# Seven block products instead of eight for chunks 12 to 15 as well, with the weight mixes made by copying and accumulating DMAs

## The chip, the cores and the metric

The kernel runs on one core of one Trainium2 chip. The metric is the device time of one execution in microseconds, lower is better. Several executions are taken and their median is given; one more is profiled.

## What is computed

The reference is a linear attention with decaying state (4 sequences, 8 heads, 768 steps, head size 48), followed by a mixture of four experts, each a two-layer network, over all 3072 rows:

```python
for t in range(S):                       # r, k, v: [4, 8, 768, 48]
    cur = einsum('bhd,bhe->bhde', u * kt, vt)
    y[:, :, t] = einsum('bhd,bhde->bhe', rt, state + cur)
    state = w * state + einsum('bhd,bhe->bhde', kt, vt)

p = domain_probs / (domain_probs.sum(-1, keepdims=True) + 1e-09)
for e in range(4):                       # x: y as [3072, 384]
    h = maximum(x @ w1[e], 0)            # [3072, 1024]
    out += p[:, e:e+1] * (h @ w2[e])     # [3072, 384]
```

## The kernel before

**Chunks and groups.** The 768 steps of each of the 4 sequences are cut into 6 chunks of 128 rows, so there are 24 chunks; chunk `ci` is step block `ci // 4` of sequence `ci % 4`. Attention runs chunk by chunk: K and R are scaled by powers of the decay (`scale`, VectorE), transposed (by a DMA transpose from chunk 8 on), multiplied into scores (`At`, TensorE), masked (`mask`, VectorE), multiplied with V (`Y`, TensorE) and completed with a diagonal term (`ruk`, `dv`, GpSimd; `Yout`, VectorE). A state update (`Sm` on TensorE, `Sv` on VectorE, `S` on GpSimd) feeds the chunk four places later. The experts work on groups of four chunks, `sc` = 0 to 5.

**The standard expert.** For groups 0 to 3 (`FIRST = 4`), layer one (`hT_ps`, lines 640 and 646) makes the hidden rows transposed, ScalarE applies ReLU (line 657), layer two (`out_ps`, line 678) takes 8 matmuls of 384 columns for each chunk and expert, and ScalarE (first expert) or VectorE (line 689, the other three) weighs the result by `p` and adds it into the output tile `oacc`.

**The seven-product form.** For groups 4 and 5 the weight `p` is multiplied into the attention row instead (`Xs`, lines 533 and 535, four scaled copies of a chunk; since `p` is not negative, ReLU lets it through). Then layer two is one product with the four experts joined in the contraction, and `products` (called for each pair of chunks, `q` = 0 or 1) makes it by a scheme of the Strassen kind: two chunks times two column halves of 192, with the contraction split in even and odd blocks. Seven products replace eight; each is 16 matmuls of 192 columns (`M_ps`, line 807), in two halves `hf` of two experts. Five of the seven need a sum or difference of hidden blocks (`sum`, line 790, 10 for each pair, VectorE), which is held in one of eight buffers S0 to S7 (four lie in the former staging area, four in the `RK` tiles of attention). Five need a mixed weight (`mix`, line 741, VectorE, one for each of 4 experts): mixes 6, 7 and 1 go into free input tiles, mixes 3 and 4 overwrite a quarter of `w2_sb`. The results are added into `oacc` on VectorE (lines 822 and 834) and copied there on ScalarE (line 828). All seven products of a group wait until layer one of the whole group is done, since the hidden rows of all four experts are needed; they then fill the whole tile `hAll`.

**The order of work.** Every piece is a job with a name, the engines that may do it with a booked time, what it needs, a rank (lower goes first) and slots that it takes or drops. A simulation in the kernel's Python code plays all jobs at the booked times and so gives the order in which each engine's instructions are issued; on the chip each engine runs its own list in order and waits on semaphores. `GATES` names for each pair of chunks from 8 on the layer-one job before which its attention may not begin. Loads are issued from SP in a fixed order, and stores, transposes and the other DMAs are on SP's queue too.

```python
job(("mix", e, what), {"V": 0.62}, run, needs, TOTC + 0.1 * e, (("inp", TOTC + e),) if tag else ())
```

Here `{"V": 0.62}` is the engine and the booked time. `("inp", ...)` is a slot of the input tiles.

Of the kernel before, what the change touches and what calls it, by code (L numbers as in the profile page):

```python
# [14 lines left out]
ALU = mybir.AluOpType  # L15
# [4 lines left out]
def kernel(  # L20
# [65 lines left out]
    spin_in = consts.tile([128, 128], BF16)  # L86
# [35 lines left out]
    for b in range(B):  # L122
        for i in range(2):
# [3 lines left out]
    wC = consts.tile([128, NP], F32)  # L127
    p_nat = consts.tile([128, E, TOTC], F32)
# [8 lines left out]
    GATES = (3, 5, 6, 7, 9, 10, 11, 12)  # L137
# [9 lines left out]
    FIRST = 4  # L147
# [4 lines left out]
                 mm=4, xTe=3, hTs=3, oacc=6, Yse=1)  # L152
    slots.update({f"{n}{i}": 1 for n, m in (("xTs", 2), ("h", 4), ("S", 8)) for i in range(m)})
# [178 lines left out]
    def attention(ci):  # L332
# [55 lines left out]
        job(("Vb", ci), {"A": 0.42} if ci < SUB else {"P": 0.5}, vb, [("Vt", ci)],  # L388
# [121 lines left out]
        def yout():  # L510
            if plain:
                tl["Ysb", ci] = work.tile([128, HD], BF16, tag="Ysb", bufs=3, name="Ysb")
# [9 lines left out]
        if dmat and plain:  # L522
            job(("Xout", ci), {"S": 1.2}, lambda: nc.sync.dma_start_transpose(
                get_xTe(sc)[:, :, ci % B, :], tl["Ysb", ci]), [("Yout", ci)], -5.0,
                (("xTe", sc),), (("Ysb", ci),), (0.45, 24))
        elif dmat:
            n_p = b * NCH + c

            def xs(e):
                def run(eng):  # L530
                    o = y_e[:, e * HD:(e + 1) * HD]
                    if eng == "A":
                        nc.scalar.mul(o, tl["Ysb", ci], p_nat[:, e, n_p:n_p + 1])
                    else:
                        nc.vector.tensor_scalar(o, tl["Ysb", ci], scalar1=p_nat[:, e, n_p:n_p + 1],  # L535
                                                scalar2=None, op0=ALU.mult)
                return run
            for e in range(E):
                job(("Xs", ci, e), {"A": 0.61, "V": 0.51}, xs(e), [("Yout", ci)] + all_cast, rk - 0.7,
                    (("Yse", ci),) if e == 0 else (), (("dv", ci),), behind=(("Xs", ci, 0),) if e else ())  # L540
            job(("Xout", ci), {"S": 1.3}, lambda: nc.sync.dma_start_transpose(
                get_xTe(sc)[:, :, ci % B, :], y_e),
                [("Xs", ci, e) for e in range(E)] + all_cast, -5.0,
                ((f"xTs{sc % 2}", sc),), (("Yse", ci),), (1.8, 96))
        else:
            tag = "mm" if ci < SUB else "tr"

            def x():
                ps = tl["X", ci] = psum.tile([128, NDB, 128], BF16, tag=tag,
                                             bufs=4 if tag == "mm" else 1, name="xT_ps")  # L550
                for db in range(NDB):
                    nc.tensor.transpose(ps[:, db, :], tl["Ysb", ci][:, db * 128:(db + 1) * 128], ident)  # L552
            job(("X", ci), {"T": 0.17}, x, [("Yout", ci)], on_pe - 1, ((tag, "X", ci),), (("Ysb", ci),))
# [18 lines left out]
        def sv():  # L572
            ps = tl["Sp", ci]
            if c:
                a = 1664 + ci % 2 * NP * D
                tl["Tn", ci] = early[:, a:a + NP * D].rearrange("p (q d) -> p q d", d=D)
# [15 lines left out]
        if c == 0:  # L592
            job(("S", ci), {"V": 0.56}, sv, [("Sm", ci), ("Yout", SUB - 1)], rk + 2, (), (("ys", "S", ci),))
        else:
            job(("Sv", ci), {"V": 0.56}, sv, [("Sm", ci)], rk - 0.1, (), (("ys", "S", ci),))
            job(("S", ci), {"P": 1.1}, sp, [("Sv", ci)], rk - 0.5)

    y_e = stg_b[:, 16384:16384 + E * HD]
# [27 lines left out]
    def moe(k, e, sc, single):  # L626
# [4 lines left out]
        for g, (fb, s0, n) in enumerate(groups):  # L631
# [19 lines left out]
            def relu(fb=fb, s0=s0, n=n):  # L651
# [10 lines left out]
                [("S", ci) for ci in range(TOTC - 2 * SUB, TOTC - SUB) if sc == FIRST and not e] +  # L662
# [48 lines left out]

    def oacc(ci):
        if ("oacc", ci // 2) not in tl:
            tl["oacc", ci // 2] = big.tile([128, 2, Dm], F32, tag="oacc", bufs=6, name="oacc")
        return tl["oacc", ci // 2][:, ci % 2, :]

    def store(ci, needs, a=0, bb=Dm):
        job(("st", ci, a), {"S": 0.5}, lambda: nc.sync.dma_start(
            out[row0(ci):row0(ci) + C, a:bb], oacc(ci)[:, a:bb]), needs, -6.0, (),
# [7 lines left out]
    def mix(e, what):  # L727
        v = b_of(e)
        B11, B12, B21, B22 = (v[:, :, j, h * DH:(h + 1) * DH] for j in range(2) for h in range(2))
        x, y, op = {1: (B11, B22, ALU.add), 6: (B11, B12, ALU.add), 7: (B21, B22, ALU.add),  # L730
                    3: (B12, B22, ALU.subtract), 4: (B21, B11, ALU.subtract)}[what]
        tag = {6: "Rt", 7: "Kt", 1: "Vt"}.get(what)

        def run(eng):
            if tag:
                o = work.tile([128, H, D], F32, tag=tag, bufs=NIN, name=tag)
                o = tl["mix", e, what] = o.rearrange("p h d -> p (h d)").bitcast(BF16).rearrange(
                    "p (i d) -> p i d", d=DH)
            else:
                o = x  # L740
            (nc.vector if eng == "V" else nc.gpsimd).tensor_tensor(o, x, y, op=op)
        needs = [("cast", 2, e, i) for i in range(NPC)]
        if what in (3, 4):
            needs += [("mix", e, 9 - what if what == 3 else 7)]
            needs += [("l2", e, ci) for ci in range(FIRST * SUB)]
        else:
            needs += [("Vt", TOTC - 1), ("Xout", TOTC - 1)]
        job(("mix", e, what), {"V": 0.62}, run, needs, TOTC + 0.1 * e, (("inp", TOTC + e),) if tag else ())

    for e in range(E):  # L750
        for what in (6, 7, 1, 3, 4):
            mix(e, what)
# [7 lines left out]
    s_no, s_tok = [0], {}  # L760
    s_free = [("T", ci, 1) for ci in range(TOTC - NRK, TOTC)]

    def products(sc, q, at0):
# [3 lines left out]
        def a_of(j, s, hf):  # L767
            return hAll[:, (1 - hf) * 2 * NFB + j:(2 - hf) * 2 * NFB:2, s, :]

        SUMS = {1: ((0, s1), (1, s2), ALU.add), 2: ((0, s2), (1, s2), ALU.add),  # L770
                5: ((0, s1), (1, s1), ALU.add), 6: ((0, s2), (0, s1), ALU.subtract),
                7: ((1, s1), (1, s2), ALU.subtract)}
# [3 lines left out]
        for n, m in enumerate(ORDER_P):  # L776
            at = at0 + 2.0 * n / 7
            for hf in range(2):
                needs = list(relus[hf])
                if m in SUMS:  # L780
                    x, y, op = SUMS[m]
                    no = s_no[0] % 8
                    s_no[0] += 1
                    if no < 4:
                        S = stg_b[:, 12288 + no * 1024:12288 + (no + 1) * 1024]
                    else:
                        S = RKB[no - 4].rearrange("p i h d -> p (i h d)")
                    S = tl["S", sc, q, m, hf] = S.rearrange("p (i c) -> p i c", c=128)
                    job(("sum", sc, q, m, hf), {"V": 0.74},
                        lambda S=S, x=x, y=y, op=op, hf=hf: nc.vector.tensor_tensor(  # L790
                            S, a_of(*x, hf), a_of(*y, hf), op=op),
                        relus[hf] + all_cast + s_free, at - 60, ((f"S{no}", sc, q, m, hf),), hts[hf])
                    s_tok[sc, q, m, hf] = (f"S{no}", sc, q, m, hf)
                    needs = [("sum", sc, q, m, hf)]
                w_ready = [("mix", e, m) for e in (2 * hf, 2 * hf + 1)] if m not in (2, 5) else []

                def mm(m=m, hf=hf):
# [14 lines left out]
                    behind=(("P", sc, q, m, 0),) if hf else ())  # L812
# [30 lines left out]
            elif m == 5:  # L843
                job(("C", sc, q, 5, 0), {"V": 0.33}, add(0, 0, ALU.subtract), ready + [("C", sc, q, 1, 0)], r, (), drop)
                job(("C", sc, q, 5, 1), {"V": 0.33}, add(0, 1, ALU.add), ready + [("C", sc, q, 3, 0)], r, (), drop)
# [217 lines left out]
```

## Time and profile before

| | us |
|---|---|
| median of 3 runs | 292.45 (291.52 to 294.41) |
| profiled execution, own time | 291.22 |
| its span, first to last instruction | 289.4 |
| TensorE busy | 282.9 (98%) |
| VectorE busy | 196.2 (68%) |
| ScalarE busy | 155.8 (54%) |
| GpSimd busy | 106.0 (37%) |

The span leaves out 1.8 us of the profiled execution's own time. A busy figure adds the durations of the engine's instructions. Matmuls overlap in TensorE's pipeline, so a group's mean duration (326 ns for a matmul of 384 columns) is longer than the distance from one start to the next; for a sum of work, the distance (the pitch) is the figure to use. In the lines, L with a number is a line of the kernel before; PE is TensorE, PEld its weight load, DVE is VectorE, ACT is ScalarE, POOL is GpSimd, SP is SyncE.

### The profile page before, as it was taken

The numbers are of one execution on the slowest core, as the hardware profiler recorded it, in microseconds if no ns is written. First come the engines' busy times: TensorE is split into PE (matmuls) and PEld (weight loads), VectorE is DVE, ScalarE is ACT, GpSimd is POOL, SyncE is SP. The second block draws the span as 40 slices with busy tenths as digits, with TensorE's granted clock in tenths as the row PEclk, the third lists the DMA queues.
The fourth block names the chain that finished last, engine by engine and source line by source line (L and its number), as shares of the span: only waits on it lengthen the run. The fifth ranks groups of instructions, "written<-read, shape, count | busy, mean of one in ns | idle before, by whom it ended". The sixth has DMA issues, their size and how long they took to land.

```text
span 289.4 us, 6324 instructions
## 1 busy us (share of the span) xinstructions
PE 282.9 (98%) x2482; PEld 181.0 (63%) x2482; DVE 196.2 (68%) x382; ACT 155.8 (54%) x262; POOL 106.0 (37%) x138
## 2 busy tenths in 40 slices
PE   7989999999999999999999999999999999999995
PEld 3777556865955554555555655555544699544995
DVE  5977976797569969674989875554793387120883
ACT  4673968647845243455455466554469701689210
POOL 2875244564979695667567132000000000000000
PEclk9999999999999999999999999999999999999999
DMA  7999999999995898979399556223110001100011
GB/s 152 248 283 271 320 305 269 187 316 202 239 184 112 158 223 191 209 159 179 79 187 194 121 127 111 57 51 60 54 57 0 0 29 40 45 1 2 0 57 54
DMA packets 120418, 40.05 MB, mean 138 GB/s; under 512 B 108458, under 2 KB 120364, under 8 KB 120388
## 3 DMA queue, kind: packets, MB, share of 16 engines
q1 hardware_dynamic: 120372, 39.64, 59.1%
q8 instruction: 19, 0.31, 0.4%
q14 instruction: 11, 0.09, 0.1%
q10 hardware_dynamic: 16, 0.00, 0.0%
HBM read 26.79 MB, written 4.72 MB: 109 GB/s over the span
## 4 chain that ended last, share of the span: by engine, by line
PE 91%; SPq 4%; DMA 3%; issue 0%; DVE 0%; ACT 0%
PE hT_ps L646 38%; PE out_ps L678 28%; PE M_ps L807 13%; PE hT_ps L640 5%; SPq L201 3%; DMA Vt<-in_v_dram 3%; PE At_ps L463 2%; PE Y_ps L501 2%; PE Y_ps L494 1%; PE St_ps L567 1%; SPq L214 1%; DMA xTe<-Ysb 1%; PE RKT_ps L421 1%; PE xT_ps L552 0%; PE p_ps L309 0%
## 5 line engine op out<-in xcount | busy, mean ns | idle before, releaser
L657 ACT ACTIVATE hAll<-hT_ps 128x512 bf16<-128x512 f32 x168 | 99.6, 597 | 73.2 <-PE hT_ps L646 67.7
L678 PE MATMUL out_ps<-w_sb,hAll 128*128 128x384 bf16 x512 | 92.9, 326 | 0.0
L646 PEld LDWEIGHTS <-w_sb 128*128 128x128 bf16 x504 | 46.9, 98 | 49.9 <-DMA xTe<-Ysb 0.8
L646 PE MATMUL hT_ps<-xTe,w_sb 128*128 128x512 bf16 x312 | 77.0, 379 | 0.3 <-DMA xTe<-Ysb 0.3
L678 PEld LDWEIGHTS <-hAll 128*128 128x128 bf16 x512 | 48.6, 98 | 34.0
L689 DVE SCALAR_TENSOR_TENSOR oacc<-out_ps,p_nat,oacc 128x384 f32<-128x384 f32 x48 | 29.4, 616 | 26.2 <-PE out_ps L678 25.6
L646 PE MATMUL hT_ps<-stg,w_sb 128*128 128x512 bf16 x192 | 42.4, 379 | 0.0
L372 POOL TENSOR_TENSOR ruk<-Rt,Kt 128x384 f32<-128x384 f32 x24 | 25.1, 1048 | 30.8 <-DMA Rt<-in_r_dram 17.8
L472 DVE TENSOR_TENSOR AtM<-At_ps,mask 128x512 bf16<-128x512 f32 x48 | 30.7, 681 | 1.4 <-PE At_ps L463 1.3
L398 POOL TENSOR_TENSOR dv<-Vt,dcoef 128x384 f32<-128x384 f32 x24 | 21.3, 889 | 15.3 <-DVE stg L535 7.4
L790 DVE TENSOR_TENSOR RK<-hAll 128x1024 bf16<-128x1024 bf16 x20 | 13.1, 686 | 18.7 <-ACT hAll L657 18.6
L380 POOL TENSOR_TENSOR ruk<-ruk,U_sd 128x384 f32<-128x384 f32 x23 | 25.2, 1097 | 0.8
L588 POOL TENSOR_TENSOR S<-hAll,wC 64x192 bf16<-64x192 f32 x32 | 17.4, 545 | 9.7 <-DVE hAll L583 8.5
L790 DVE TENSOR_TENSOR stg<-hAll 128x1024 bf16<-128x1024 bf16 x20 | 13.1, 686 | 9.7 <-ACT hAll L657 9.5
L640 PE MATMUL hT_ps<-xTe,w_sb 128*128 128x128 bf16 x288 | 18.0, 219 | 0.4 <-ACT w_sb L78 0.2
L640 PEld LDWEIGHTS <-w_sb 128*128 128x128 bf16 x288 | 16.6, 98 | 1.0 <-ACT w_sb L78 0.4
L82 POOL CAST Vb<-Vt 128x384 bf16<-128x384 f32 x20 | 11.6, 581 | 13.6 <-DMA Vt<-in_v_dram 5.3
L359 DVE TENSOR_TENSOR RK<-Kt,W_sd 128x384 bf16<-128x384 f32 x20 | 16.5, 830 | 0.0
L655 ACT ACTIVATE hAll<-hT_ps 128x512 bf16<-128x512 f32 x24 | 14.1, 596 | 4.2 <-PE hT_ps L640 3.3
L687 ACT ACTIVATE oacc<-out_ps,p_nat 128x384 f32<-128x384 f32 x16 | 9.2, 579 | 12.5 <-PE out_ps L678 8.8
L393 DVE TENSOR_REDUCE dcoef<-ruk 128x8 f32<-128x384 f32 x24 | 13.1, 545 | 3.4 <-POOL ruk L380 3.0
L828 ACT COPY oacc<-M_ps 128x384 f32<-128x384 f32 x8 | 3.8, 479 | 19.6 <-PE M_ps L807 19.6
(89 smaller groups left out, 298.4 us busy)
## 6 DMA issues: line engine op xcount, KB each, us to landing
stg<-in_moe_w_dram SPq DMA_DIRECT2D x16, 576.0 KB, 6.6
Kt<-in_k_dram SPq DMA_DIRECT2D x24, 192.0 KB, 3.8
Vt<-in_v_dram SPq DMA_DIRECT2D x24, 192.0 KB, 3.9
Rt<-in_r_dram SPq DMA_DIRECT2D x24, 192.0 KB, 4.3
out_dram<-oacc SPq DMA_DIRECT2D x23, 192.0 KB, 1.9
stg<-in_moe_w_dram SPq DMA_DIRECT2D x8, 384.0 KB, 6.6
RKT<-RK SPq DMA_TRANSPOSE x16, 3.3
out_dram<-oacc SPq DMA_DIRECT2D x2, 96.0 KB, 1.6
```

The source lines that it names most:

```text
L372: nc.gpsimd.tensor_mul(tl["ruk", ci], tl["Rt", ci], tl["Kt", ci])
L380: nc.gpsimd.tensor_mul(tl["ruk", ci], tl["ruk", ci], U_sd)
L398: nc.gpsimd.tensor_mul(tl["dv", ci], tl["Vt", ci], tl["dcoef", ci].to_broadcast((128, H, D)))
L472: nc.vector.tensor_mul(tl["AtM", ci][:, j], tl["At", ci, j], mask[:, None, :].to_broadcast((128, NP, C)))
L588: nc.gpsimd.tensor_mul(S_new[pr, :, cl], tl["Tn", ci][pr], wC[pr, :, None].to_broadcast((P2, NP, D)))
L640: nc.tensor.matmul(ps[:, i, :], w1_sb[:, e, db, (fb + i) * 128:(fb + i + 1) * 128], xTe[:, db, s0, :], start=(i == 0 and db == 0), stop=(i ...
L646: nc.tensor.matmul(ps[:, 0:n, :].rearrange("p a b -> p (a b)"), w1_sb[:, e, db, fb * 128:(fb + 1) * 128], xTe[:, x0 + db, s0:s0 + n, :].re ...
L657: nc.scalar.activation(hTs[:, fb, s0:s0 + n, :], ps[:, 0:n, :], AF.Relu)
L678: nc.tensor.matmul(ps, relu_tile(e, sc)[:, fb, s, :], w2_sb[:, e, fb, :], start=(fb == 0), stop=(fb == NFB - 1))
L689: nc.vector.scalar_tensor_tensor(oacc(ci), in0=tl["o", e, ci], scalar=pe, in1=oacc(ci), op0=ALU.mult, op1=ALU.add)
L790: lambda S=S, x=x, y=y, op=op, hf=hf: nc.vector.tensor_tensor(S, a_of(*x, hf), a_of(*y, hf), op=op),
L807: nc.tensor.matmul(tl["P", sc, q, m], st, moving(m, e, i), start=(hf == 0 and n == 0), stop=(hf == 1 and n == 7))
```

## The change

Group 3 (chunks 12 to 15) goes over to the seven-product form: `FIRST` becomes 3. The signs of the scheme are turned: all sums of hidden blocks become differences, and four of the five weight mixes become sums, which a DMA can make by adding into its destination. A mix is now made for two experts at once. Mix 1 stays on VectorE as a difference. Mixes 7 and 6 are made by a copying DMA from SP and an accumulating DMA from GpSimd, both within SBUF, into output tiles and layer-one input tiles that are free by then. Mixes 4 and 3 are accumulated in place in `w2_sb` by one DMA from GpSimd each, once the standard layer two of groups 0 to 2 is done with the experts concerned.

Around it: in the new group the sums have six buffers, four in the staging area, one in the `Ysb` tiles and one in an output tile (the `RK` tiles are still in use by attention then); the sums for the first pair are ordered with four of them ahead. All sums are chained in a fixed order, and so are all products. The state's temporary `Tn` gets its own tile, the gates of five pairs of chunks move, V copies from chunk 8 on may be made on ScalarE too, and the scaled copies `Xs` rank later.

```diff
-    GATES = (3, 5, 6, 7, 9, 10, 11, 12)
+    GATES = (3, 6, 6, 3, 9, 11, 13, 15)
-    FIRST = 4
+    FIRST = 3
+    MIX_RANK = 13.0
+    XS_ON = {"A": 0.61, "V": 0.51}
+    MIX_ON = {"V": 1.5}
+    VB_ON = {'A': 0.42, 'P': 0.5}
+    XS_RANK = 1.0
+    SUM_RANK = -60
...
-        job(("Vb", ci), {"A": 0.42} if ci < SUB else {"P": 0.5}, vb, [("Vt", ci)],
+        job(("Vb", ci), {"A": 0.42} if ci < SUB else {"P": 0.5} if ci < 8 else VB_ON, vb, [("Vt", ci)],
...
-                [("S", ci) for ci in range(TOTC - 2 * SUB, TOTC - SUB) if sc == FIRST and not e] +
...
+    o_sb = weights.tile([128, 6, 2, Dm], F32)
+    o_free, o_at, o_left = list(range(6)), {}, {}
...
+    def mix_by_dma(what, hf):
+        home = ({1: 0, 7: 1, 6: 2}.get(what), hf)
+        where = None if what in (3, 4) else "oacc" if home in ((0, 0), (0, 1), (1, 0)) else "xTe"
+        j1, h1, j2, h2 = quarters(what)
+        both = w2_sb[:, 2 * hf:2 * hf + 2].rearrange("p e (i j) d -> p (e i) j d", j=2)
+        x, y = (both[:, :, j, h * DH:(h + 1) * DH] for j, h in ((j1, h1), (j2, h2)))
...
+        cast = [("cast", 2, e, i) for e in (2 * hf, 2 * hf + 1) for i in range(NPC)]
+        if where == "oacc":
+            needs = cast + [("ev", E - 1, ci) for ci in range(2 * SUB)]
         else:
+            needs = cast + [("l1", E - 1, FIRST - 1 if home == (2, 1) else 1, NFB - 1, 0)]
+        if what == 1:
+            job(("mix", 1, hf), MIX_ON, lambda eng: (nc.vector if eng == "V" else nc.gpsimd).tensor_tensor(
+                out_of(), x, y, op=ALU.subtract), needs, MIX_RANK, ((where, "mix", home),))
+            return
+        if where:
+            job(("mixc", what, hf), {"S": 0.5}, lambda: nc.sync.dma_start(out_of(), x), needs, 900.0,
+                ((where, "mix", home),), (), (2.6, 64))
+            needs = [("mixc", what, hf)]
+        else:
+            needs = [("mix", 6 if what == 3 else 7, hf)]
+            needs += [("l2", e, ci) for ci in range(FIRST * SUB) for e in (2 * hf, 2 * hf + 1)]
+        job(("mix", what, hf), {"P": 1.2}, lambda eng: nc.gpsimd.dma_start(
+            out_of() if where else x, y, accum_op=ALU.add), needs, MIX_RANK)
+
+    for what in (1, 7, 6, 4, 3):
+        for hf in range(2):
+            mix_by_dma(what, hf)
...
+        homes = (0, 1, 2, 3, 8, 9) if sc == FIRST else (0, 1, 2, 3, 4, 5, 6, 7)
+        ahead = 0 if q else len(homes) - 2
+        seq_s = [(m, 0) for m in with_sum[:ahead]]
+        for n, m in enumerate(with_sum):
+            seq_s += [(m, 1)] if ahead else [(m, 0), (m, 1)]
+            if ahead and n + ahead < len(with_sum):
+                seq_s.append((with_sum[n + ahead], 0))
...
+                lambda S=S, x=x, y=y, key=(sc, q, m, hf): nc.vector.tensor_tensor(
+                    s_of(S, key), a_of(*x, key[3]), a_of(*y, key[3]), op=ALU.subtract),
...
-                w_ready = [("mix", e, m) for e in (2 * hf, 2 * hf + 1)] if m not in (2, 5) else []
+                w_ready = [("mix", m, hf)] if m not in (2, 5) else []
```

More of the change, by code (lines that the diff above doesn't have):

```diff
@@ L85 @@
     nc.scalar.preload_act_table_set("natural_log_exp_and_others")
-    spin_in = consts.tile([128, 128], BF16)
+    spin_in = early[:, 1664:1728].bitcast(BF16)
     nc.vector.memset(spin_in, 1.0)
@@ L127 @@
     wC = consts.tile([128, NP], F32)
+    Tn = consts.tile([128, NP, D], F32)
     p_nat = consts.tile([128, E, TOTC], F32)
@@ L151 @@
     slots = dict(inp=NIN, wst=NST, RKT=4, AtM=2, Ysb=3, ruk=3, dv=3, Vb=4, At=2, tr=1, ys=1,
-                 mm=4, xTe=3, hTs=3, oacc=6, Yse=1)
-    slots.update({f"{n}{i}": 1 for n, m in (("xTs", 2), ("h", 4), ("S", 8)) for i in range(m)})
+                 mm=4, xTe=3, hTs=3, oacc=6, Yse=1, Tn=1)
+    slots.update({f"{n}{i}": 1 for n, m in (("xTs", 2), ("h", 4), ("S", 10)) for i in range(m)})
     jobs = {}
@@ L511, in yout @@
             if plain:
-                tl["Ysb", ci] = work.tile([128, HD], BF16, tag="Ysb", bufs=3, name="Ysb")
+                y_at[ci] = y_free.pop(0)
+                tl["Ysb", ci] = y_sb[:, y_at[ci] * HD:(y_at[ci] + 1) * HD]
             else:
@@ L522, in attention, with x_dma @@
         if dmat and plain:
-            job(("Xout", ci), {"S": 1.2}, lambda: nc.sync.dma_start_transpose(
-                get_xTe(sc)[:, :, ci % B, :], tl["Ysb", ci]), [("Yout", ci)], -5.0,
+            def x_dma():
+                nc.sync.dma_start_transpose(get_xTe(sc)[:, :, ci % B, :], tl["Ysb", ci])
+                y_free.append(y_at[ci])
+            job(("Xout", ci), {"S": 1.2}, x_dma, [("Yout", ci)], -5.0,
                 (("xTe", sc),), (("Ysb", ci),), (0.45, 24))
@@ L538, in attention @@
             for e in range(E):
-                job(("Xs", ci, e), {"A": 0.61, "V": 0.51}, xs(e), [("Yout", ci)] + all_cast, rk - 0.7,
+                job(("Xs", ci, e), XS_ON, xs(e), [("Yout", ci)] + all_cast, rk + XS_RANK,
                     (("Yse", ci),) if e == 0 else (), (("dv", ci),), behind=(("Xs", ci, 0),) if e else ())
@@ L552, in x @@
                     nc.tensor.transpose(ps[:, db, :], tl["Ysb", ci][:, db * 128:(db + 1) * 128], ident)
+                y_free.append(y_at[ci])
             job(("X", ci), {"T": 0.17}, x, [("Yout", ci)], on_pe - 1, ((tag, "X", ci),), (("Ysb", ci),))
@@ L574, in sv @@
             if c:
-                a = 1664 + ci % 2 * NP * D
-                tl["Tn", ci] = early[:, a:a + NP * D].rearrange("p (q d) -> p q d", d=D)
+                tl["Tn", ci] = Tn
             for j in range(2):
@@ L594, in attention @@
         else:
-            job(("Sv", ci), {"V": 0.56}, sv, [("Sm", ci)], rk - 0.1, (), (("ys", "S", ci),))
-            job(("S", ci), {"P": 1.1}, sp, [("Sv", ci)], rk - 0.5)
+            job(("Sv", ci), {"V": 0.56}, sv, [("Sm", ci)], rk - 0.1, (("Tn", ci),), (("ys", "S", ci),))
+            job(("S", ci), {"P": 1.1}, sp, [("Sv", ci)], rk - 0.5, (), (("Tn", ci),))
+    y_sb = weights.tile([128, 3 * HD], BF16)
+    y_free, y_at = [0, 1, 2], {}
     y_e = stg_b[:, 16384:16384 + E * HD]
@@ L710, in moe, with run @@
                 store(ci, [("ev", e, ci)])
+    o_sb = weights.tile([128, 6, 2, Dm], F32)
+    o_free, o_at, o_left = list(range(6)), {}, {}
     def oacc(ci):
         if ("oacc", ci // 2) not in tl:
-            tl["oacc", ci // 2] = big.tile([128, 2, Dm], F32, tag="oacc", bufs=6, name="oacc")
+            o_at[ci // 2] = o_free.pop(0)
+            tl["oacc", ci // 2] = o_sb[:, o_at[ci // 2]]
         return tl["oacc", ci // 2][:, ci % 2, :]
     def store(ci, needs, a=0, bb=Dm):
-        job(("st", ci, a), {"S": 0.5}, lambda: nc.sync.dma_start(
-            out[row0(ci):row0(ci) + C, a:bb], oacc(ci)[:, a:bb]), needs, -6.0, (),
+        o_left[ci // 2] = o_left.get(ci // 2, 0) + 1
+        def run():
+            nc.sync.dma_start(out[row0(ci):row0(ci) + C, a:bb], oacc(ci)[:, a:bb])
+            o_left[ci // 2] -= 1
+            if not o_left[ci // 2]:
+                o_free.append(o_at[ci // 2])
+        job(("st", ci, a), {"S": 0.5}, run, needs, -6.0, (),
             (("oacc", ci // 2),), (0.5 if bb - a == Dm else 0.3, 8))
@@ L725, in b_of @@
         return w2_sb[:, e].rearrange("p (i j) d -> p i j d", j=2)
[L727 to L745, printed above, removed]
-        else:
-            needs += [("Vt", TOTC - 1), ("Xout", TOTC - 1)]
-        job(("mix", e, what), {"V": 0.62}, run, needs, TOTC + 0.1 * e, (("inp", TOTC + e),) if tag else ())
@@ L750, with quarters, out_of @@
-    for e in range(E):
-        for what in (6, 7, 1, 3, 4):
-            mix(e, what)
+    def quarters(what):
+        return {1: (0, 0, 1, 1), 6: (0, 0, 0, 1), 7: (1, 0, 1, 1), 3: (0, 1, 1, 1), 4: (1, 0, 0, 0)}[what]
+    def mix_by_dma(what, hf):
[4 more added lines that the diff above has]
+        x, y = (both[:, :, j, h * DH:(h + 1) * DH] for j, h in ((j1, h1), (j2, h2)))
+        def out_of():
+            if ("mixed", home) not in tl:
+                if where == "oacc":
+                    u = o_sb[:, o_free.pop(0)].rearrange("p s d -> p (s d)").bitcast(BF16)
+                else:
+                    u = big.tile([128, NDB, SUB, 128], BF16, tag="xTe", bufs=3, name="w_mix")
+                    u = u.rearrange("p a s c -> p (a s c)")
+                tl["mixed", home] = u.rearrange("p (i d) -> p i d", d=DH)
+                for i in range(2):
+                    tl["mix", 2 * hf + i, what] = tl["mixed", home][:, 4 * i:4 * i + 4, :]
+            return tl["mixed", home]
+        cast = [("cast", 2, e, i) for e in (2 * hf, 2 * hf + 1) for i in range(NPC)]
+        if where == "oacc":
+            needs = cast + [("ev", E - 1, ci) for ci in range(2 * SUB)]
+        else:
+            needs = cast + [("l1", E - 1, FIRST - 1 if home == (2, 1) else 1, NFB - 1, 0)]
[7 more added lines that the diff above has]
+            needs = [("mixc", what, hf)]
+        else:
+            needs = [("mix", 6 if what == 3 else 7, hf)]
+            needs += [("l2", e, ci) for ci in range(FIRST * SUB) for e in (2 * hf, 2 * hf + 1)]
+        job(("mix", what, hf), {"P": 1.2}, lambda eng: nc.gpsimd.dma_start(
+            out_of() if where else x, y, accum_op=ALU.add), needs, MIX_RANK)
@@ L758, in moving @@
         return {2: v[:, i, 0, 0:DH], 3: v[:, i, 0, DH:Dm], 4: v[:, i, 1, 0:DH], 5: v[:, i, 1, DH:Dm]}[m]
-    s_no, s_tok = [0], {}
+    s_no, s_tok, s_last, p_last = [0] * NSC, {}, [None], [None]
+    y_over = [("Xout", ci) for ci in range(FIRST * SUB)]
     s_free = [("T", ci, 1) for ci in range(TOTC - NRK, TOTC)]
@@ L768, in a_of @@
             return hAll[:, (1 - hf) * 2 * NFB + j:(2 - hf) * 2 * NFB:2, s, :]
-        SUMS = {1: ((0, s1), (1, s2), ALU.add), 2: ((0, s2), (1, s2), ALU.add),
-                5: ((0, s1), (1, s1), ALU.add), 6: ((0, s2), (0, s1), ALU.subtract),
-                7: ((1, s1), (1, s2), ALU.subtract)}
+        SUMS = {1: ((0, s1), (1, s2)), 2: ((0, s2), (1, s2)), 5: ((0, s1), (1, s1)),
+                6: ((0, s2), (0, s1)), 7: ((1, s1), (1, s2))}
         relus = [[("relu", e, sc, fb, 0) for e in (2 * hf, 2 * hf + 1) for fb in range(NFB)]
@@ L775, in products @@
         hts = [tuple((h_tag(e, sc), e, sc) for e in (2 * hf, 2 * hf + 1)) for hf in range(2)]
-        for n, m in enumerate(ORDER_P):
-            at = at0 + 2.0 * n / 7
-            for hf in range(2):
[L779 to L794, printed above, removed]
-                w_ready = [("mix", e, m) for e in (2 * hf, 2 * hf + 1)] if m not in (2, 5) else []
@@ new lines, in products @@
+        homes = (0, 1, 2, 3, 8, 9) if sc == FIRST else (0, 1, 2, 3, 4, 5, 6, 7)
+        at_of = {m: at0 + 2.0 * n / 7 for n, m in enumerate(ORDER_P)}
+        with_sum = [m for m in ORDER_P if m in SUMS]
+        ahead = 0 if q else len(homes) - 2
[4 more added lines that the diff above has]
+                seq_s.append((with_sum[n + ahead], 0))
@@ new lines, in s_of @@
+        def s_of(S, key):
+            if S is None:
+                if "s_pair" not in tl:
+                    tl["s_pair"] = o_sb[:, o_free.pop(0)].rearrange("p s d -> p (s d)").bitcast(BF16)[:, 0:1024]
+                S = tl["S", *key] = tl["s_pair"].rearrange("p (i c) -> p i c", c=128)
+            return S
+        for m, hf in seq_s:
+            x, y = SUMS[m]
+            no = homes[s_no[sc] % len(homes)]
+            s_no[sc] += 1
+            if no < 4:
+                S = stg_b[:, 12288 + no * 1024:12288 + (no + 1) * 1024]
+            elif no < 8:
+                S = RKB[no - 4].rearrange("p i h d -> p (i h d)")
+            else:
+                S = y_sb[:, 0:1024] if no == 8 else None
+            if S is not None:
+                S = tl["S", sc, q, m, hf] = S.rearrange("p (i c) -> p i c", c=128)
+            job(("sum", sc, q, m, hf), {"V": 0.74},
+                lambda S=S, x=x, y=y, key=(sc, q, m, hf): nc.vector.tensor_tensor(
+                    s_of(S, key), a_of(*x, key[3]), a_of(*y, key[3]), op=ALU.subtract),
+                relus[hf] + all_cast + (s_free if 4 <= no < 8 else y_over if no == 8 else []),
+                at_of[m] + SUM_RANK, ((f"S{no}", sc, q, m, hf),) + ((("oacc", "S"),) if no == 9 else ()), hts[hf],
+                behind=(s_last[0],) if s_last[0] else ())
+            s_last[0] = ("sum", sc, q, m, hf)
+            s_tok[sc, q, m, hf] = (f"S{no}", sc, q, m, hf)
@@ L797, in mm @@
+        for m in ORDER_P:
+            at = at_of[m]
+            for hf in range(2):
+                needs = [("sum", sc, q, m, hf)] if m in SUMS else list(relus[hf])
+                w_ready = [("mix", m, hf)] if m not in (2, 5) else []
                 def mm(m=m, hf=hf):
@@ L811, in products @@
                     hts[hf] + ((s_tok[sc, q, m, hf],) if m in SUMS else ()),
-                    behind=(("P", sc, q, m, 0),) if hf else ())
+                    behind=(p_last[0],) if p_last[0] else ())
+                p_last[0] = ("P", sc, q, m, hf)
             def o_of(m=m):
@@ L843, in products @@
             elif m == 5:
-                job(("C", sc, q, 5, 0), {"V": 0.33}, add(0, 0, ALU.subtract), ready + [("C", sc, q, 1, 0)], r, (), drop)
-                job(("C", sc, q, 5, 1), {"V": 0.33}, add(0, 1, ALU.add), ready + [("C", sc, q, 3, 0)], r, (), drop)
+                job(("C", sc, q, 5, 0), {"V": 0.33}, add(0, 0, ALU.add), ready + [("C", sc, q, 1, 0)], r, (), drop)
+                job(("C", sc, q, 5, 1), {"V": 0.33}, add(0, 1, ALU.subtract), ready + [("C", sc, q, 3, 0)], r, (), drop)
             elif m == 7:
```

## The prediction

> **What bounds the kernel now.** I read the page from the top: busy shares, the rows of 40 slices, the chain that ended last; then the chain in order of time for the last third, the stretches cut at its borders, and the groups of the lines that the diff touches.
>
> ```profile
> PE 282.9 (98%) x2482; PEld 181.0 (63%) x2482; DVE 196.2 (68%) x382; ACT 155.8 (54%) x262; POOL 106.0 (37%) x138
> ...
> PE   7989999999999999999999999999999999999995
> ...
> PE 91%; SPq 4%; DMA 3%; issue 0%; DVE 0%; ACT 0%
> ```
>
> A busy TensorE alone proves little, so the chain is read next: 91% of it is TensorE, and from 109 us on there is nothing else until the last addition.
>
> ```profile
> 211.20 1.30 PE out_ps L678 x8
> 212.50 16.19 PE hT_ps L646 x75
> 228.68 18.48 PE M_ps L807 x224
> 247.16 20.72 PE hT_ps L646 x96
> 267.88 18.50 PE M_ps L807 x224
> 286.38 0.02 issue
> 286.40 0.35 DVE oacc L822
> ```
>
> Columns: start, length, what, how many. Each block's length over its count is the pitch: 20.72 / 96 = 215.8 ns (512 columns), 18.48 / 224 = 82.5 ns (192 columns), 1.30 / 8 = 162.5 ns (384 columns). Both seven-product blocks have the same pitch throughout, so TensorE never waits for a sum or a mixed weight there. The waits of TensorE agree: none over 1.1 us, and that one is at the start. So the end moves by the matmul time taken out, less any new TensorE stall.
>
> The other engines, cut at the same borders (PE, PEld, DVE, ACT, POOL busy, clock, DMA share, GB/s):
>
> ```profile
> 130.00:170.00 40.00, 40.00 (x338) 22.71 (x335) 32.46 (x62) 20.90 (x37) 21.45 (x30) 1.00 0.72 144
> 170.00:212.50 42.50, 42.50 (x277) 23.09 (x276) 24.43 (x47) 23.45 (x41) 3.46 (x5) 1.00 0.38 78
> 212.50:228.68 16.18, 16.18 (x77) 7.39 (x76) 7.33 (x14) 14.32 (x24) 0.00 (x0) 1.00 0.04 13
> 228.68:247.16 18.48, 18.48 (x226) 18.42 (x224) 14.46 (x29) 2.51 (x5) 0.00 (x0) 1.00 0.09 34
> ```
>
> VectorE is the second busiest: 81% while attention and standard layers run, 78% in a seven-product block. Today those two never meet: GpSimd has done with attention at 178 us, the first such block starts at 228.68. After the change they do meet.
>
> **What the Trainium skill says.** (1) "TensorE: Matmul & The Clock Gate", Back-to-back issue gap, gives N / 2.4 + 2.5 ns for warm matmuls in isolation and warns that weight loads can make it longer at small N; the trace has 82.5 and 162.5 ns, the formula's 82.5 and 162.5, with no such penalty. (2) "DMA: Bandwidth & Descriptors", SWDGE vs HWDGE vs iDMA: an accumulating transfer can only be issued from GpSimd, whose cores write the descriptors; the section Anatomy of one DMA fits about 2.0 us + bytes / 436 kB per us. No transfer of the kernel before is of this kind, so nothing here confirms it. (3) "SBUF — State Buffer", Who interferes with whom: a VectorE instruction with two SBUF inputs shuts out GpSimd reads. The trace agrees in kind: the GpSimd product L380 runs from 992 to 1512 ns. (4) The DMA page's rules for kernel authors: another access to the bytes of an accumulate must wait for its semaphore. So products 3 and 4 cannot start before their in-place transfers land.
>
> **The change part by part.**
>
> *TensorE.* Chunks 12 to 15 lose the standard second layer, 4 chunks x 4 experts x 8 = 128 matmuls at 162.5 ns = 20.80 us, and gain 2 pairs x 7 products x 16 = 224 at 82.5 ns = 18.48 us. Saved: 2.32 us. Layer one and attention keep their counts. No stall of size is left to recover after the start (the trace shows one of 0.4 us near 109 us), so 2.3 us is close to the most that the change can give.
>
> *ScalarE.* Out: 4 first evictions at 579 ns (L687), 2.3 us. In: 4 copies at 479 ns and its share of 16 scalings at 606 ns (L533). In the pure layer-one stretch it has 14.32 of 16.18 us busy, nearly all ReLU (24 at 597 ns); work put there would delay TensorE through the four PSUM buffers. The scalings of chunks 12 to 15 come earlier, where ScalarE is half idle (20.90 of 40): I cost them at nothing. Without that cover each would be 0.6 us.
>
> *VectorE.* Out: 12 additions at 616 ns = 7.4 us, and 20 mixes at 551 ns = 11.0 us. In: 20 sums at 686 ns = 13.7 us; result additions 12 x 352 + 2 x 554 ns = 5.3 us; two mixes of doubled size, estimated from the 551 ns row at 1.0 us each; up to 16 scalings at 412 ns = 6.6 us, less ScalarE's share. Sum about +5 us of 196: harmless as a total. The place matters. When the last chunk of 8 to 11 has left the second layer, TensorE has three experts of layer one left, 24 x 648 ns = 15.5 us, then the 18.5 us block. In the 15.5 us VectorE has four advance sums (2.7), attention of chunks 20 and 21 and their scalings. One chunk there costs 0.83 + 0.72 (scale) + 2 x 0.68 (mask) + 0.55 + 0.55 = 4.0 us, its scalings 1.6 if all here: 14.0 of 15.5. In the block: the 14.5 us of today's block, of 18.5. Chunks 22 and 23 want another 11.3 us. Over both stretches 39.8 us of work stands against 34.0, and 5.8 must slide into the following layer-one stretch, where today's twin of it has only 2.85 us of VectorE work in 20.7. It may slide: these chunks are not read until layer one of chunks 20 to 23, some 40 us later, and sums outrank attention (SUM_RANK -60). Only six sum buffers instead of eight stand in this block; walking the order, a sum needs the buffer of a product two ahead, and each arrives 0.3 us or more before use. I take 1 us of stalls for the block, bounds 0 and 4.
>
> *Weight mixes.* Ten jobs for two experts each: two on VectorE, four copies from SP, eight accumulations from GpSimd (for 7, 6, 4 and 3). Each transfer has 128 x 8 runs of 384 bytes, 1024 packets, as many as an input load (192 kB in 192-byte runs).
>
> ```profile
> q1 hardware_dynamic: 120372, 39.64, 59.1%
> ...
> Kt<-in_k_dram SPq DMA_DIRECT2D x24, 192.0 KB, 3.8
> ```
>
> 0.591 x 16 x 289.4 us / 120372 = 22.7 ns a packet; 64 packets an engine = 1.5 us, landing at 3.8. An accumulation reads two and writes one: low bound like a plain load, 3.8 us; high bound twice the packet time and GpSimd held throughout, 1.5 + 3.8 = 5.3 us each with the next one behind it. The skill's fit gives 2.0 + 393 / 436 = 2.9 us. I take 4.5 us to landing and about 1.2 us on GpSimd (the figure that the diff's plan books; bounds 1.0 and 5.3). For mixes 7 and 6 this is hidden: used 15 us or more later. Mixes 4 and 3 for experts 2 and 3 may start only after that last second-layer matmul, so 15.5 us before use; two in a row take under 10. On GpSimd, 4 x 1.2 = 4.8 us join 21.45 of 40; ahead of a dv or S there, an issue delays Y, but the wait has room. The copies stand last in SP's order, behind loads and transposes. SP also carries four transposes of four times the size for chunks 12 to 15; a DMA share of 0.72 leaves room.
>
> *The rest.* The gates let chunks 20 to 23 begin only with layer one of chunks 12 to 15 (experts 1 and 3), near 170 and 180 us; today their score matmuls run at 163 and 186 us. Their rows are wanted at about 245, so the delay costs nothing unless it crowds the block (C). V copies of chunks 8 to 23 (0.5 us) may go to ScalarE; it has room there. Removing the 24-fold wait on old S jobs, the fixed Tn tile, the hand-kept y_sb and o_sb: bookkeeping. Four of six output slots go to mixes and sums; two pairs then share two slots 20 us apart, and a store takes 1.9 us.
>
> Sum: 291.22 - 2.3 + 1.0 = 289.9 for the profiled execution; the median of the runs shown lies 1.23 above it: 291.2 us.
>
> **Rivals.**
> *VectorE full (C).* If attention of chunks 22 and 23 lands inside the block instead of sliding, 14.5 + 8.0 = 22.5 us stand against 18.5: 4 us of stall at worst, about 3 with part of it elsewhere. For it: 78% today without any attention. Against: the ranks. 292.45 - 2.3 + 3 = 293.1.
> *Accumulations late (B), the slower side.* Place: between the last second-layer matmul of chunks 8 to 11 and product 3. If the four in-place accumulations run one behind the other on GpSimd, the point of decision is 15.5 / 4 = 3.9 us each. At the 5.3 bound the last lands 21.2 us after, 5.7 late; with smaller stalls through GpSimd before, 6.5: 292.45 - 2.3 + 6.5 = 296.7. For it: the plan counts the mixed weight as there 0.17 us after the issue, which no transfer of the page does. Against: experts 0 and 1 are free earlier, so only two need stand in line.
>
> **How the numbers follow.** Forecast 0.48, C 0.24, B 0.28. A measurement of this kernel tells about 1%, 2.9 us, from no change. The forecast lies within it, apart from 0.04 beyond on the fast side, since 2.3 saved can hardly be 2.9. C is within for 0.16 and slower for 0.08. B is slower. Faster 0.04, same 0.60, slower 0.36. Range: from 289.6, full saving and a little more, to 298.5, B with some GpSimd delay on top. The forecast's own range is 289.8 to 292.6.
>
> **What would show it.** 672 matmuls at L807's successor with 82.5 ns pitch, 384 at L678's; a block of 224 near 187 to 206 us lasting 18.5 us plus its stalls. Waits of TensorE on VectorE sums in this block speak for C; waits on an accumulating DMA before the first product for B; GpSimd instructions over 1.2 us at the DMA issues would break my price. Stalls of TensorE before 165 us would mean that the new order of attention costs what I took as free, and that the forecast is wrong.

## The result, and the profile after

The changed kernel takes 312.38 us (median of 4 runs, 310.87 to 313.06), the kernel before 292.43 us beside it: ratio 1.0665, interval 1.0597 to 1.0733. The forecast of 291.2 us was wrong by 21 us, outside its range. The profiled execution took 312.0 us, 20.8 more than before. A ratio is formed from the undisturbed runs of both kernels, so it can differ a little from the quotient of the medians given.

The page of the changed kernel, for the rows shown of before (line numbers are from here on those of the kernel that ran):

```profile
PE 287.1 (93%) x2555; PEld 189.3 (61%) x2578; DVE 201.0 (65%) x395; ACT 164.0 (53%) x283; POOL 111.8 (36%) x132
...
PE   8989999999999999499993897599999999999995
...
PEclk9999999999999999979999599789999999999999
...
PE 76%; DMA 9%; SPq 5%; POOL 3%; DVE 3%; issue 2%; ACT 0%; POOLq 0%; ACTq 0%
```

TensorE has three holes (the 4, the 3 and the 7 5 of its row, near 128, 165 and 190 to 199 us), and its granted clock drops at each of them. In the kernel before it never moved in the middle:

```profile
PEclk9999999999999999999999999999999999999999
```

The chain is TensorE for 76% instead of 91%, and 9% of it is DMA. What TensorE waited for:

```profile
PE At_ps L470 <- DMA RKT<-RK: 7.2, 3, 4.3
PE out_ps L689 <- ACT hAll L669: 5.5, 1, 5.5
PE hT_ps L658 <- ACT hAll L669: 2.7, 1, 2.7
```

Columns: total us, times, longest. The kernel before had one wait for a DMA:

```profile
PE hT_ps L646 <- DMA xTe<-Ysb: 0.3, 1, 0.3
```

Score matmuls wait for the DMA transpose of attention (`RKT`), and expert matmuls wait for ReLU (`hAll`), which is not slow itself: in ScalarE's list a row scaling stands ahead of it, and that waits for a DMA. The chain in order of time shows it:

```profile
124.42 7.77 DMA RKT<-RK
132.19 0.05 issue
132.23 0.40 PE At_ps L470 x8
...
161.86 0.61 PE hT_ps L658 x3
162.47 7.56 DMA stg<-stg
170.03 0.02 issue
170.06 0.02 ACTq L543
170.07 0.04 issue
170.12 0.62 ACT stg L543
170.73 0.49 ACT hAll L669
171.22 0.04 issue
171.27 2.72 PE out_ps L689 x8
...
192.17 6.74 DMA RKT<-RK
```

All three are transposes on SP's queue that land 6.7 to 7.8 us after their start. The last eight matmuls of the second piece take 2.72 us instead of 1.30: half clock. Beside each such transpose stand accumulations: they are issued at 116.9 and 118.7 us, at 151.7 to 157.1 and at 178.2 to 185.5. The view of DMA queues and issues:

```profile
q1 hardware_dynamic: 129140, 42.40, 63.5%
q0 software_dynamic: 8320, 3.15, 11.2%
...
w_sb<-w_sb POOLq DMA_DIRECT2D x4, 384.0 KB, 10.1
...
w_mix<-w_sb POOLq DMA_DIRECT2D x3, 384.0 KB, 8.8
...
o_sb<-w_sb POOLq DMA_DIRECT2D x1, 384.0 KB, 9.6
```

Columns of the first two lines: packets, MB, share of the time of 16 engines; of the others: KB of one transfer, and median us from the issue to the landing, when all data are there. The software queue of GpSimd has 1040 packets for each of eight accumulations. Its share times the span, 0.112 x 16 x 310.2 us / 8320, is 66.8 ns a packet; the hardware queue has 24.4 ns. The packet times of one accumulation add up to 0.112 x 310.2 / 8 = 4.3 us of all 16 DMA engines, its engine time below (packets can overlap: from 160 to 175 us the shares of both queues add up to 1.24). It lands after 8.8 to 10.1 us. Beside accumulations the other queue can nearly stand: from 160 to 165 us the trace has about 1760 packets of the software queue and 230 of the hardware queue, from 165 to 170 us, as the accumulations end, about 310 and 3620. SP feels it too: issuing one scaled-row transpose holds it for up to 5.9 us, against 2.2 before, and all that stands behind it in SP's list waits.

The sum: waits of TensorE 7.2 + 5.5 + 2.7 = 15.4 us; three half-clock stretches of 3.4, 6.8 and 6.8 us, in which TensorE was busy for 14.7 us, half of which, 7.3 us, is lost; less the 2.3 us saved. That is 20.4 us of the 20.8 found.

The new seven-product block itself runs well (PE, PEld, DVE, ACT, POOL busy, clock, DMA share, GB/s):

```profile
208.55:227.69 19.14, 19.14 (x241) 18.81 (x240) 16.25 (x32) 4.49 (x9) 0.38 (x1) 1.00 0.38 87
```

Of the 19.14 us, 0.55 us are score matmuls of chunks 22 and 23; the products keep their pitch: 18.59 us instead of 18.48.

### The profile page after: what moved, and what is told of

Its sections match the earlier page's. It is cut to its first block, busy times and chain, and to the rows that moved or that the text cites. A ratio compares the mean times of both kernels' runs of the same rounds, so it can differ in the third digit from the quotient of the medians.

```text
span 310.2 us, 6512 instructions
## 1 busy us (share of the span) xinstructions
PE 287.1 (93%) x2555; PEld 189.3 (61%) x2578; DVE 201.0 (65%) x395; ACT 164.0 (53%) x283; POOL 111.8 (36%) x132
## 3 DMA queue, kind: packets, MB, share of 16 engines
q0 software_dynamic: 8320, 3.15, 11.2%
## 4 chain that ended last, share of the span: by engine, by line
PE 76%; DMA 9%; SPq 5%; POOL 3%; DVE 3%; issue 2%; ACT 0%; POOLq 0%; ACTq 0%
PE hT_ps L658 29%; PE out_ps L689 18%; PE M_ps L866 18%; DMA RKT<-RK 5%; PE hT_ps L652 4%; DMA stg<-stg 2%; SPq L208 2%; DMA Rt<-in_r_dram 2%; PE At_ps L470 2%; POOL S L598 1%; POOL dv L405 1%; PE Y_ps L508 1%; PE Y_ps L501 1%; SPq L221 1%; SPq L412 1%
## 5 line engine op out<-in xcount | busy, mean ns | idle before, releaser
L689 PE MATMUL out_ps<-w_sb,hAll 128*128 128x384 bf16 x384 | 72.0, 334 | 5.5 <-ACT hAll L669 5.5
L658 PE MATMUL hT_ps<-stg,w_sb 128*128 128x512 bf16 x279 | 67.1, 392 | 3.3 <-ACT hAll L669 2.7
L689 PEld LDWEIGHTS <-hAll 128*128 128x128 bf16 x384 | 36.8, 99 | 31.0 <-issue 8.1
L658 PE MATMUL hT_ps<-xTe,w_sb 128*128 128x512 bf16 x202 | 52.4, 382 | 0.7
L843 DVE TENSOR_TENSOR stg<-hAll 128x1024 bf16<-128x1024 bf16 x38 | 25.0, 687 | 16.3 <-ACT hAll L669 12.5
L700 DVE SCALAR_TENSOR_TENSOR o_sb<-out_ps,p_nat,o_sb 128x384 f32<-128x384 f32 x36 | 21.9, 613 | 16.9 <-PE out_ps L689 16.7
L866 PEld LDWEIGHTS <-stg 128*128 128x128 bf16 x304 | 25.3, 98 | 0.1
L598 POOL TENSOR_TENSOR S<-Tn,wC 64x192 bf16<-64x192 f32 x32 | 22.2, 694 | 6.6 <-DVE Tn L593 5.2
L543 ACT ACTIVATE stg<-dv,p_nat 128x384 bf16<-128x384 f32 x20 | 11.7, 608 | 16.5 <-DMA stg<-stg 16.1
L866 PE MATMUL M_ps<-w_sb,hAll 128*128 128x192 bf16 x192 | 16.8, 246 | 0.0
## 6 DMA issues: line engine op xcount, KB each, us to landing
w_sb<-w_sb POOLq DMA_DIRECT2D x4, 384.0 KB, 10.1
```

Of the source, the lines that this page charges most:

```text
L598: nc.gpsimd.tensor_mul(S_new[pr, :, cl], tl["Tn", ci][pr], wC[pr, :, None].to_broadcast((P2, NP, D)))
L658: nc.tensor.matmul(ps[:, 0:n, :].rearrange("p a b -> p (a b)"), w1_sb[:, e, db, fb * 128:(fb + 1) * 128], xTe[:, x0 + db, s0:s0 + n, :].re ...
L689: nc.tensor.matmul(ps, relu_tile(e, sc)[:, fb, s, :], w2_sb[:, e, fb, :], start=(fb == 0), stop=(fb == NFB - 1))
L700: nc.vector.scalar_tensor_tensor(oacc(ci), in0=tl["o", e, ci], scalar=pe, in1=oacc(ci), op0=ALU.mult, op1=ALU.add)
L843: lambda S=S, x=x, y=y, key=(sc, q, m, hf): nc.vector.tensor_tensor(s_of(S, key), a_of(*x, key[3]), a_of(*y, key[3]), op=ALU.subtract),
L866: nc.tensor.matmul(tl["P", sc, q, m], st, moving(m, e, i), start=(hf == 0 and n == 0), stop=(hf == 1 and n == 7))
```

## The experiments

Theory: the accumulations occupy the DMA engines, and the transposes that TensorE waits for come late; the halved clock follows. Rivals: the new form for chunks 12 to 15 (four times larger transposes, a single buffer for scaled rows, VectorE); GpSimd held by issuing.

### Accumulations cut to an eighth

```diff
-            out_of() if where else x, y, accum_op=ALU.add), needs, MIX_RANK)
+            (out_of() if where else x)[:, 0:1, :], y[:, 0:1, :], accum_op=ALU.add), needs, MIX_RANK)
```

> The eight accumulating transfers move one of the eight runs of each partition (the rest of the addition is left out); every engine's instruction order is that of the changed kernel. Theory (the 1040 packets of each accumulation, at 67 ns each, hold the DMA engines and delay the transposes that TensorE waits for): the three stalls of TensorE of 4.5, 5.7 and 6.1 us and the half-clock stretches after them go, 289 to 293 us. Rival (the four times larger transposes of chunks 12 to 15 and the single scaled-row buffer set the delay, whatever the accumulations carry): stays above 305 us. Second rival (GpSimd held by issuing, 1.6 us each): between, above 298 us, since the issues stay.

Measured: 289.51 us, ratio to before 0.9907 (0.9884 to 0.993). The whole loss is gone, and the kernel is 2.4 us faster than before at 291.93: the 2.3 us of the prediction's sum. All else of the change is in it: order, gates, larger transposes, eight issues on GpSimd, four copies from SP. So the first rival is out. The last pieces of its chain, as after the change but 23 us earlier:

```profile
226.28 18.48 PE M_ps L866 x224
244.76 20.72 PE hT_ps L658 x96
265.48 18.50 PE M_ps L866 x224
```

The transposes of attention are back at what they took before (the lines of before and of the changed kernel stand further down):

```profile
DMA to landing us min/median/max: 3.1/3.6/4.9
```

The issue on GpSimd is also shorter, 0.87 us instead of 1.56; this run alone does not part that from the engine time of the packets. The runs with half of each accumulation and with long runs do.

### Plain copies of the same runs

```diff
-            out_of() if where else x, y, accum_op=ALU.add), needs, MIX_RANK)
+            out_of() if where else x, y), needs, MIX_RANK)
```

> The eight transfers from GpSimd become plain copies of the same runs (the addition is left out); same instruction order on every engine. If the accumulate operation is what is dear: packets at 20 to 30 ns instead of 67, landing near 4 to 5 us, 290 to 296 us. If the software queue of GpSimd is what is dear, whatever it carries: packets stay above 50 ns and the time above 305 us.

Measured: 293.06 us, 1.0022 (0.9998 to 1.0047); its twenty runs spread from 291.08 to 307.77. In the two longest the granted clock is 0.98 on average, which points to stalls there as well; the trace is of a run of 291.72 us, without a stall over 1.1. The queue line:

```profile
q0 software_dynamic: 896, 3.15, 4.8%
```

The same bytes need 896 packets instead of 8320: in a plain copy the runs are joined to packets of 3456 and 4224 bytes, in the accumulation each run of 384 bytes stays a packet. The forecast of 20 to 30 ns a packet was therefore wrong, 248 ns is what comes out, but each carries nine runs or more. Engine time for a transfer: 0.048 x 289.9 / 8 = 1.7 us instead of 4.3; landing 4.8 to 5.7 us. Accumulating short runs, not the software queue as such, is dear; yet even copies take back the saving.

### The new form with all mixes on VectorE

```diff
-            job(("mixc", what, hf), {"S": 0.5}, lambda: nc.sync.dma_start(out_of(), x), needs, 900.0,
...
-        job(("mix", what, hf), {"P": 1.2}, lambda eng: nc.gpsimd.dma_start(
-            out_of() if where else x, y, accum_op=ALU.add), needs, MIX_RANK)
+        job(("mix", what, hf), MIX_ON, lambda eng: nc.vector.tensor_tensor(
+            out_of() if where else x, x, y, op=ALU.subtract if what == 1 else ALU.add), needs, MIX_RANK,
+            ((where, "mix", home),) if where else ())
```

> Seven products for chunks 12 to 15 as in the change, but all ten weight mixes on VectorE (128x1536, about 1 us each) and no copying or accumulating transfer. The order of work is planned anew. Theory of the accumulations: near 290 to 294 us, the saving of 2.3 us less some VectorE crowding of 0 to 4 us. Rival (the seven products for chunks 12 to 15 themselves crowd VectorE, SP and the scaled rows): above 300 us.

Measured: 289.76 us, 0.994 (0.9912 to 0.9967). This version beats both kernels, the one before by 0.6%, without a transfer for the mixes. The view of groups has the ten mixes at 1.07 to 1.09 us each:

```profile
L777 DVE TENSOR_TENSOR w_sb<-w_sb 128x1536 bf16<-128x1536 bf16 x4 | 4.2, 1091 | 0.0
...
L777 DVE TENSOR_TENSOR w_mix<-w_sb 128x1536 bf16<-128x1536 bf16 x3 | 3.2, 1077 | 0.0
```

The stretch with the new block, cut in the same way as before:

```profile
184.00:206.00 22.00, 21.99 (x256) 20.06 (x255) 19.88 (x40) 5.94 (x12) 2.13 (x3) 1.00 0.32 76
```

VectorE is 90% busy there (19.88 of 22.00) and TensorE has no hole. The ten mixes run earlier, between 114 and 170 us, where VectorE is busy for 46.3 of 56 us; it had room for them after all.

### The transfers alone, with the old four groups

```diff
-    GATES = (3, 6, 6, 3, 9, 11, 13, 15)
+    GATES = (3, 5, 6, 7, 9, 10, 11, 12)
-    FIRST = 3
+    FIRST = 4
```

> The weight mixes by copying and accumulating transfers alone: seven products only for chunks 16 to 23 and the gates of the kernel before. Theory of the accumulations: slower than before by 5 to 15 us, 297 to 307 us, with waits of TensorE on transposes. Rival (chunks 12 to 15 in the new form are the cause): within 2 us of before.

Measured: 307.26 us, 1.0526 (1.0479 to 1.0572), just above the upper end of the expectation and far beyond the rival's. The chain in order of time again has transposes, two of attention and two of scaled rows:

```profile
121.71 9.03 DMA RKT<-RK
...
139.10 9.11 DMA RKT<-RK
...
204.65 10.21 DMA stg<-stg
...
233.75 7.54 DMA stg<-stg
```

With the third experiment this parts the change into its two halves: products -0.6%, transfers +5.3% (without the products). The second half is not quite pure: the new ranks, buffers and chained orders stay in it, and the transfers run at other times than in the change. The first and third experiments contain these too, without a loss.

### Half of each accumulation

```diff
-            out_of() if where else x, y, accum_op=ALU.add), needs, MIX_RANK)
+            (out_of() if where else x)[:, 0:4, :], y[:, 0:4, :], accum_op=ALU.add), needs, MIX_RANK)
```

> The eight accumulating transfers move four of the eight runs of each partition (half of the addition is left out); same instruction order. Theory (the cost grows with the accumulated packets, and what a transpose can wait without harm is used up first): between 291 and 303 us, nearer the lower end, since half of 9 us to landing fits the slack of most transposes. Rival (a fixed cost for each accumulating transfer above some small size): within 4 us of the changed kernel's 312.

Measured: 290.83 us, 0.9961 (0.9932 to 0.999), just under the expected range (before, beside it: 291.76 us). By the ratios, half costs 0.5% over the eighth and the second half another 7%. A fixed cost is out, and so is issuing on GpSimd as the whole cause, since it still takes 1.28 us here. Engine time for a transfer is 0.056 x 291.4 / 8 = 2.0 us, landing 5.1 to 6.1 us. The plan's slack covers such delays and not twice them.

### The same bytes in long runs

```diff
-        job(("mix", what, hf), {"P": 1.2}, lambda eng: nc.gpsimd.dma_start(
-            out_of() if where else x, y, accum_op=ALU.add), needs, MIX_RANK)
+        job(("mix", what, hf), {"P": 1.2}, lambda eng: nc.gpsimd.dma_start((out_of() if where else tl["mixed", (2 if what == 3 else 1, hf)]).rearrange("p i d -> p (i d)"),
+            w2_sb[:, 2 * hf, 0:4, :].rearrange("p f d -> p (f d)"), accum_op=ALU.add), needs, MIX_RANK)
```

> The eight accumulating transfers keep their bytes (384 KB each) but run over one stretch of 3072 bytes in each partition, on both sides, instead of eight runs of 384 (other data are added, and the last four are added into the tiles of mixes 6 and 7 instead of in place); same instruction order on the other engines. If the cost goes by packets: engine time of each transfer falls from 4.3 us of all 16 engines to under 2, landing to under 6 us, 289 to 296 us. If it goes by bytes through the accumulate: 305 us or more, landing stays near 9 us.

Measured: 298.79 us, 1.0198 (1.0125 to 1.0272), between the two forecasts, so neither holds alone.

```profile
q0 software_dynamic: 1152, 3.15, 7.2%
```

Packets are seven times fewer, but 0.072 x 294.0 / 8 = 2.6 us of engine time for a transfer remain, 0.9 above the plain copy of as many bytes. As an estimate from these three runs, of the 4.3 us of a short-run accumulation some 1.7 go with the short runs, 0.9 with accumulating, 1.7 with the bytes. Landing took 5.6 us into the mix tiles (6.8 into output tiles), and one stall of 3 us is left near 161 us, behind a scaled-row transpose that lands after 8.57 us. GpSimd's issues take 0.87 us here, as with the eighth, yet by the ratios the kernel is 2.9% slower than the eighth, some 8.5 us: issuing is not what costs.

### Whole accumulations for mixes 6 and 7 only

```diff
-        job(("mix", what, hf), {"P": 1.2}, lambda eng: nc.gpsimd.dma_start(
-            out_of() if where else x, y, accum_op=ALU.add), needs, MIX_RANK)
+        job(("mix", what, hf), {"P": 1.2}, lambda eng: nc.gpsimd.dma_start((out_of() if where else x)[:, 0:8 if where else 1, :],
+            y[:, 0:8 if where else 1, :], accum_op=ALU.add), needs, MIX_RANK)
```

> The four accumulations for mixes 6 and 7 are whole, the four in place for mixes 3 and 4 move one run of eight (the rest is left out); same instruction order. Theory: each stall belongs to the accumulations in flight beside it. Mixes 7 start at 117 us, one of 6 at 154.5, so the stall near 128 us stays (4.5 us and a half-clock stretch), the ones near 165 and 192 us shrink or go: 294 to 302 us. Rival (the first late stretch shifts all that follows): above 306 us.

Measured: 297.39 us, 1.0196 (1.0133 to 1.0259), as expected. The first stall stays:

```profile
131.50 0.61 PE L470 MATMUL At_ps<-RKT 64*128 64x128 bf16 x8 [3.82 <-DMA RKT<-RK]
```

and a half-clock stretch of 6.8 us goes with it. The one near 165 us shrinks from 5.5 to 0.8 us, the last from 2.7 + 2.5 to under 1 us. Each stall belongs to the accumulations beside it.

| kernel | engine time of one transfer, us | latest landing of a transpose (attention, scaled rows), us | median, us | ratio to before |
|---|---|---|---|---|
| eighth | 0.5 | 4.9, 4.8 | 289.51 | 0.9907 |
| plain copy | 1.7 | 7.1, 8.6 | 293.06 | 1.0022 |
| half | 2.0 | 5.8, 7.1 | 290.83 | 0.9961 |
| long runs | 2.6 | 6.6, 9.3 | 298.79 | 1.0198 |
| the change | 4.3 | 10.6, 9.1 | 312.38 | 1.0665 |

Engine time is the queue's share times the span over eight transfers. In the kernel before, the latest landings are 5.3 and 4.7 us, with all mixes on VectorE 5.1 and 5.0. The plain copy stands a little out of line with the half, in the landings as in the time; so engine time alone does not set the delay, and what else does is open. Nor does each late landing cost: only those that TensorE waits for do.

## Why the prediction was wrong

- TensorE's saving, 2.32 us, was right: the eighth shows 2.4, and its first new block runs from 185.7 to 204.8 us, where the prediction put it. (The small stall near 109 us in the kernel before is 0.3 us, not 0.4.)
- VectorE full (C) did not happen. Its total grew by 4.8 us, as the sum said; in the block it was busy for 16.25 us of 19.14, attention included, no product waited, and the 1 us of stalls taken for the block was 0.1.
- GpSimd's issue, 1.2 us, took 1.54 at least and up to 2.2. That was too low, but of little effect.
- Accumulation to landing, "I take 4.5 us", high bound 5.3, took 8.8 to 10.1 by row and up to 12.3. The packet price was taken from loads (22.7 ns, doubled at worst); it was 66.8. The skill's fit ("DMA: Bandwidth & Descriptors", Anatomy of one DMA), 2.9 us, is far under it in this loaded kernel; even the plain copies took 4.8 to 5.7. The true value lay above both bounds.
- Rival B had the right culprit and the wrong place. Product 3 never waited for its weight, although the last in-place transfer ended only at 197 us: the block began at 208.55, TensorE having lost its time before.
- The step that failed is in the part on the mixes. "For mixes 7 and 6 this is hidden: used 15 us or more later" asks only when the mixed weights are needed, and "a DMA share of 0.72 leaves room" takes for granted what the DMA engines carry meanwhile: what an accumulation does to other transfers stood at nothing. The last experiment shows these four alone, the others cut to an eighth: by the ratios, 2.9% over the eighth. All eight, at 4.3 us each instead of 1.5 (3.0 at the high bound), are 34.7 us of all 16 engines between 117 and 197 us, beside a queue at 0.72 to 0.89 already. The transposes are the late ones: those of attention land after 10.6 us at worst, 5.3 before, those of scaled rows after 9.1, 4.7 before.
- A sign was named, stalls before 165 us, and it came, at 128 us. But it was to mean that the new order of attention costs. The eighth keeps that order on every engine and has no such stall, so this meaning was wrong.
- No term stood for the clock. A stall is paid twice here: 15.4 us of waits brought another 7 us lost at half clock.
- The half experiment shows how sharp the border was: with 2.0 us of engine time for each transfer the forecast of 291.2 would have been met.

The line of the transpose `RKT` in the kernel before:

```profile
DMA to landing us min/median/max: 3.0/3.3/5.3
```

and in the changed one:

```profile
DMA to landing us min/median/max: 3.0/3.8/10.6
```

The median hardly moves; the few that matter do.

## What to carry to other kernels

A transfer that nobody waits for soon is not free: charge its engine time to every other transfer in flight, and ask which of these a busy engine will wait for. The eight weight sums that were moved to the DMA engines cost some 22 us there; on VectorE, 73% busy with all ten, they cost nothing that was seen, since they ran where its queue had gaps. Before pricing an accumulating DMA, look at the length of its runs: those of 384 bytes here were not joined into larger packets as the plain copy's were.

## What the runs showed that was not expected

- Accumulating packets of 384 bytes took 66.8 ns each beside 24.4 ns for the hardware queue's, and these nearly stopped: 230 in 5 us, against about 3620 in the next 5 us. Whether the engines' arbitration or the memory side does this, no run here tells.
- Short stalls halved TensorE's clock. In the kernel with the transfers alone, a wait of 2.23 us was enough, and 3.4 us at half clock followed:

```profile
130.78 0.61 PE L470 MATMUL At_ps<-RKT 64*128 64x128 bf16 x8 [2.23 <-DMA RKT<-RK]
```

The stretch after it:

```profile
130.70:134.10 3.40, 3.32 (x16) 1.54 (x17) 2.35 (x5) 0.60 (x1) 0.00 (x0) 0.50 1.18 245
```

The column after the engines is the granted clock, 0.50. The Trainium skill ("TensorE: Matmul & The Clock Gate", HAM oscillation) asks for no idle gap over about 3.4 us; this one was shorter. With all mixes on VectorE, a wait of 1.8 us near 19 us left the clock at 1.00.
- Joining of runs in the software queue: 896 packets of up to 4224 bytes for a plain copy, 8320, nearly all of 384, for the same bytes accumulated.
